# Dealing the first weights' columns out to the hidden blocks by fours, so that a row of a part of the second weights is one piece

## The chip, the cores and the metric

The kernel runs on one core of one Trainium2 chip. The metric is the device time of one execution in microseconds (us). The engines are TensorE (PE in the profile, its weight loads PEld), VectorE (DVE), ScalarE (ACT), GpSimd (POOL) and SyncE (SP). A transfer between memory and the chip is issued from the queue of SyncE or GpSimd.

## The reference, cut to what matters

Sparse attention over 8 batches, 8 heads, 576 positions and 64 dimensions (four heads with a local mask, four with a strided one) makes `x` of 4608 tokens by 512. A layer with a hidden width of 2048 follows; the change is in the latter alone:

```python
def _moe_ref(x, w_in, w_out):          # x 4608x512, w_in 512x2048, w_out 2048x512
    h = x @ w_in
    alpha = 1.0
    g = np.where(h > 0.0, h, alpha * (np.exp(np.minimum(h, 0.0)) - 1.0))
    return (g @ w_out).astype(np.float32)
```

The hidden width is summed over in the second product, so its 2048 units may be numbered in any order, as long as the columns of `w_in` and the rows of `w_out` follow the same one.

## The kernel before, in words

The tokens are kept as `xT`, with the 512 features on the partitions in `KC` = 4 chunks of 128. The tokens are taken in 9 chunks (`nb`) of 512. For each chunk the hidden width is cut into `MC` = 16 blocks (`m`) of 128 units. `moe_in` makes one block of `h`: four matmuls, one for each chunk `c` of features, with the 128 columns of `w_in_sb` that belong to the block as the stationary operand (a weight load of 128 by 128) and 512 tokens of `xT` as the moving one. These go through `moe_chunk` (L622). `moe_act` (L645 to L657) takes exp on ScalarE and a minimum, a subtraction and a maximum on VectorE, and writes block `m` of `g_sb`, with the 128 units on the partitions.

`moe_out` (L667) makes the output for 128 tokens: it runs over all 16 blocks, with 128 tokens of `g_sb` as the stationary operand and row block `m` of `w_out_sb` (128 units by 512) as the moving one. A quarter of that, four blocks, is one "part" of a call. ScalarE copies the sum to `o_sb` (L671), and SyncE stores it (L673).

The order of work is written out by hand. An opening list (`OPENING`) runs batch 0 of the attention, with some matmuls of the first three blocks in it (`moe_ahead`). After that, for each `nb` and each step `s` of 16, the loop issues pieces of the attention of the next batch, `moe_in` and `moe_act` of block `s`, and one part of `moe_out`, mostly of the chunk before. For the first chunk, parts 0, 1 and 2 of the first 128 tokens come at steps 11, 13 and 15.

Both weights are converted from float32 to bf16 by the transfers that load them, on GpSimd's queue. `w_in` comes in four transfers (`load_w_in(i)`, L316) of 512 columns each, which serve blocks 4i to 4i+3. `w_out` comes in four transfers (L728), one for each four blocks. They stand behind the loads of batch 1 and the last transfer of `w_in`, and ahead of the clearings (`clear_v`, `clear_nat`) and the loads of batch 2 (`load_batch(2)`: `load_strided`, L178 and L182, and `load_local`, L189 and L195).

Row `128 m + p` of `w_out` lies on partition `p`, in block `m`. So in one of the four transfers a partition gets four rows of `w_out` that are 128 rows apart in memory:

```python
wo = moe_w_out.rearrange("(m p) d -> p m d", p=128)
```

The attention is made for pairs of heads, in steps that carry short matmuls between those of the layer: transposes (L361, L375, L571, L584), scores (L456, L493) and the product with the values (L535, 65 columns). A second path (`general_path`) runs only when a range check on the sums of the attention fails.

Of the kernel before, what the change touches and what calls it, by code (L numbers as in the profile page):

```python
# [58 lines left out]
def kernel(  # L59
# [9 lines left out]
    nc = tc.nc  # L69
# [59 lines left out]
    w_in_sb = consts.tile([128, KC, d_ff], BF16, tag="w_in_sb")  # L129
# [115 lines left out]
    def clear_v(i, engine=nc.vector):  # L245
        engine.memset(v_str[i][:, :, :, D:], 1.0)
        engine.memset(v_loc[i][0:32, :, 0, :], 0.0)
        engine.memset(v_loc[i][:, :, :, D:], 1.0)
# [61 lines left out]
    nc.vector.memset(kT["loc"][1][:, :, 0:32], 0.0)  # L310

    wi = moe_w_in.rearrange("(c p) f -> p c f", p=128)
    wo = moe_w_out.rearrange("(m p) d -> p m d", p=128)

    def load_w_in(i):
        nc.gpsimd.dma_start(out=w_in_sb[:, :, 512 * i:512 * (i + 1)],  # L316
# [302 lines left out]
    hps_of = {}  # L619

    def moe_chunk(nb, m, c, hps, start, stop):
        nc.tensor.matmul(hps, lhsT=w_in_sb[:, c, m * 128:(m + 1) * 128],  # L622
                         rhs=xT[:, c, nb * N_TILE:(nb + 1) * N_TILE],
                         start=start, stop=stop)

    def moe_ahead(c, start, stop):

        for m in range(AHEAD):
            if start:
                ahead[m] = rings["hps"].next()  # L630
            moe_chunk(0, m, c, ahead[m], start, stop)

    def moe_in(nb, m):
        if m == 0:
            g_of[nb] = p_g.tile([128, MC, N_TILE], BF16, tag="g_sb", name="g_sb")
        if nb == 0 and m in ahead:
            hps = ahead[m]
        else:
            hps = rings["hps"].next()
            order = C_ORDER if nb < EARLY else sorted(C_ORDER)  # L640
            for c in order:
                moe_chunk(nb, m, c, hps, c == order[0], c == order[-1])
        hps_of[m] = hps
# [82 lines left out]
    load_w_in(3)  # L726
    for i in range(4):
        nc.gpsimd.dma_start(out=w_out_sb[:, 4 * i:4 * (i + 1), :],  # L728
                            in_=wo[:, 4 * i:4 * (i + 1), :])
    clear_v(2, nc.gpsimd)  # L730
    clear_nat(2, nc.gpsimd)
    load_batch(2)
# [50 lines left out]

    inner.close()
    general_path(tc, q, k, v, out, w_in_sb, w_out_sb, xT, identity, flag)


def general_path(tc, q, k, v, out, w_in_sb, w_out_sb, xT, identity, flag):


    nc = tc.nc
    B, H, S, D = q.shape
    KC, MC = w_in_sb.shape[1], w_out_sb.shape[1]
    redo = nc.values_load(flag[0:1, 0:1], min_val=0, max_val=1)
    with tc.If(redo > 0):
        with (
            tc.tile_pool(name="gp_c", bufs=1) as p_c,
            tc.tile_pool(name="gp", bufs=2) as p_s,
            tc.tile_pool(name="gp_ps", bufs=1, space=PSUM) as p_ps,
        ):  # L800

            same = p_c.tile([128, S], F32, tag="same")
            other = p_c.tile([128, S], F32, tag="other")
            nc.vector.memset(same, 0.0)
            for j in range(4):
                nc.gpsimd.affine_select(same, same, compare_op=ALU.not_equal, fill=1.0,
                                        base=-STRIDE * j,
                                        pattern=[[0, S // STRIDE], [-1, STRIDE]],
                                        channel_multiplier=1)
            nc.vector.tensor_scalar(other, same, scalar1=1.0, scalar2=-NEG,  # L810
                                    op0=ALU.subtract, op1=ALU.mult)
            for b in range(B):
                for hp in range(H // 2):
                    general_pair(nc, p_s, p_ps, q, k, v, xT, identity, same, other,
                                 b, hp)
            for nb in range(B * S // 512):
                g_sb = p_c.tile([128, MC, 512], BF16, tag="g", name="g")
                for m in range(MC):
                    hps = p_ps.tile([128, 512], F32, tag="a", name="hps")
                    for c in range(KC):  # L820
                        nc.tensor.matmul(hps, lhsT=w_in_sb[:, c, m * 128:(m + 1) * 128],
                                         rhs=xT[:, c, nb * 512:(nb + 1) * 512],
                                         start=(c == 0), stop=(c == KC - 1))
                    e_sb = p_s.tile([128, 512], F32, tag="e", name="e")
                    nc.scalar.activation(e_sb, hps, ACT.Exp)
                    e1_sb = p_s.tile([128, 512], BF16, tag="e1", name="e1")
                    nc.vector.tensor_scalar(e1_sb, e_sb, scalar1=1.0, scalar2=1.0,
                                            op0=ALU.min, op1=ALU.subtract)
                    nc.vector.tensor_tensor(g_sb[:, m, :], e1_sb, hps, op=ALU.max)
                for kk in range(4):  # L830
                    ops = p_ps.tile([128, 512], F32, tag="b", name="ops")
                    for m in range(MC):
                        nc.tensor.matmul(ops, lhsT=g_sb[:, m, kk * 128:(kk + 1) * 128],
                                         rhs=w_out_sb[:, m, :], start=(m == 0),
                                         stop=(m == MC - 1))
                    o_sb = p_s.tile([128, 512], F32, tag="o", name="o")
                    nc.scalar.copy(o_sb, ops)
                    r0 = nb * 512 + kk * 128
                    nc.sync.dma_start(out=out[r0:r0 + 128, :], in_=o_sb)
# [106 lines left out]
```

## Time and profile before

| what | value |
|---|---|
| median of 3 runs | 326.81 us (326.43 to 327.97) |
| profiled execution | 327.16 us, its span 325.3 us |
| mean granted TensorE clock | 0.997 |
| TensorE busy | 301.5 us (93%) |
| VectorE, ScalarE, GpSimd busy | 243.3, 177.8, 131.4 us |
| transfers on the GpSimd queue | 67632 packets, 18.10 MB |
| transfers on the SyncE queue | 34469 packets, 17.11 MB |
| read from and written to memory | 36.70 MB, 9.44 MB |

A line of the profile's groups names the source line, the engine, the operation, the tiles (out<-in), the shape and the count; then the busy time in us and the mean of one in ns; then the idle time of the engine before it and what ended it. A line of a timeline gives the start, the time that the merged instructions took, both in us, and the count. A line of the waits gives who waited for whom, the total in us, the number of times and the longest. A matmul's recorded duration (379 ns for 512 columns) holds its way through the array too, and consecutive matmuls overlap: the distance between starts is the pace. A weight load (PEld) can run beside the matmul before it.

### The profile page before, as it was taken

The numbers are of one execution on the slowest core, as the hardware profiler recorded it, in microseconds if no ns is written. First come the engines' busy times: TensorE is split into PE (matmuls) and PEld (weight loads), VectorE is DVE, ScalarE is ACT, GpSimd is POOL, SyncE is SP. The second block draws the span as 40 slices with busy tenths as digits, with TensorE's granted clock in tenths as the row PEclk, the third lists the DMA queues.
The fourth block names the chain that finished last, engine by engine and source line by source line (L and its number), as shares of the span: only waits on it lengthen the run. The fifth ranks groups of instructions, "written<-read, shape, count | busy, mean of one in ns | idle before, by whom it ended". The sixth has DMA issues, their size and how long they took to land.

```text
span 325.3 us, 6088 instructions
## 1 busy us (share of the span) xinstructions
PE 301.5 (93%) x2205; PEld 150.8 (46%) x2246; DVE 243.3 (75%) x539; ACT 177.8 (55%) x337; POOL 131.4 (40%) x208
## 2 busy tenths in 40 slices
PE   2697888999999999999999999999999999999992
PEld 1463544555544554444444454454445444444440
DVE  6576887787888788988798879887887666866600
ACT  3577885776455664555555655555565444434320
POOL 9579825958389368839823830000000000000000
PEclk9999999999999999999999999999999999999998
DMA  6999999999999999999988992920210001100012
GB/s 112 154 169 120 168 207 139 148 130 162 158 141 97 106 154 172 139 182 169 148 117 143 148 135 62 153 83 35 55 48 32 33 34 54 43 35 33 32 67 72
DMA packets 102138, 35.67 MB, mean 110 GB/s; under 512 B 79885, under 2 KB 97493, under 8 KB 102101
## 3 DMA queue, kind: packets, MB, share of 16 engines
q0 software_dynamic: 67632, 18.10, 64.6%
q1 hardware_dynamic: 34469, 17.11, 24.8%
q8 instruction: 19, 0.31, 0.4%
q14 instruction: 18, 0.15, 0.2%
HBM read 36.70 MB, written 9.44 MB: 142 GB/s over the span
## 4 chain that ended last, share of the span: by engine, by line
PE 86%; DVE 4%; DMA 3%; ACT 3%; issue 2%; POOL 2%; ACTq 0%; POOLq 0%
PE single L667 38%; PE half L622 28%; PE single L622 9%; PE single L535 3%; DMA k_loc<-in_k_dram 3%; PE pair_a L456 2%; PE single L375 2%; PE single L571 1%; ACT e_sb L648 1%; PE pair_a L493 1%; DVE g_sb L657 1%; POOL k_str L178 1%; DVE x_l L544 1%; DVE x_s L544 1%; DVE g_sb L652 1%
## 5 line engine op out<-in xcount | busy, mean ns | idle before, releaser
L667 PE MATMUL single<-w_out_sb,g_sb 128*128 128x512 bf16 x558 | 143.6, 379 | 1.4 <-DVE g_sb L657 0.4
L622 PE MATMUL half<-xT,w_in_sb 128*128 128x512 bf16 x419 | 110.3, 379 | 1.1 <-issue 0.3
L648 ACT ACTIVATE e_sb<-half 128x512 f32<-128x512 f32 x109 | 65.3, 599 | 68.7 <-PE half L622 62.4
L655 DVE TENSOR_SCALAR e_sb<-e_sb 128x512 bf16<-128x512 f32 x139 | 62.0, 446 | 36.5 <-ACT e_sb L648 35.4
L667 PEld LDWEIGHTS <-g_sb 128*128 128x128 bf16 x576 | 53.5, 98 | 59.6 <-DVE g_sb L657 1.2
L622 PEld LDWEIGHTS <-w_in_sb 128*128 128x128 bf16 x576 | 51.7, 98 | 55.2 <-issue 0.2
L657 DVE TENSOR_TENSOR g_sb<-e_sb,half 128x512 bf16<-128x512 bf16 x104 | 71.5, 688 | 3.6
L622 PE MATMUL single<-xT,w_in_sb 128*128 128x512 bf16 x136 | 36.0, 379 | 0.3 <-issue 0.2
L648 ACT ACTIVATE e_sb<-single 128x512 f32<-128x512 f32 x35 | 21.1, 602 | 21.6 <-PE single L622 19.6
L671 ACT COPY o_sb<-single 128x512 f32<-128x512 f32 x36 | 21.1, 586 | 17.7 <-PE single L667 16.5
L535 PEld LDWEIGHTS <-pr 128*128 128x128 bf16 (+3 forms) x352 | 20.9, 105 | 15.0 <-issue 1.1
L178 POOL DMA_DIRECT2D v_raw<-in_v_dram x32 | 19.9, 659 | 15.8 <-DVE v_str L414 15.7
L462 ACT ACTIVATE pr<-pair_a 126x936 bf16<-126x936 f32 (+1 forms) x20 | 19.2, 962 | 11.8 <-PE single L456 11.8
L657 DVE TENSOR_TENSOR g_sb<-e_sb,single 128x512 bf16<-128x512 bf16 x35 | 24.1, 688 | 1.2
L178 POOL DMA_DIRECT2D k_str<-in_k_dram x32 | 20.1, 647 | 7.6 <-issue 3.6
L178 POOL DMA_DIRECT2D q_str<-in_q_dram x28 | 17.6, 651 | 6.3 <-DMA w_out_sb<-in_moe_w_out_dram 2.0
L544 DVE TENSOR_TENSOR x_l<-single,rden 96x384 bf16<-96x384 f32 x32 | 17.7, 554 | 1.1
L501 ACT ACTIVATE pr<-pair_a 128x576 bf16<-128x576 f32 (+2 forms) x20 | 13.1, 653 | 6.9 <-PE pair_a L493 6.9
L544 DVE TENSOR_TENSOR x_s<-single,rden 126x256 bf16<-126x256 f32 (+1 forms) x32 | 15.7, 491 | 1.1
L543 DVE RECIPROCAL rden<-single 96x6 f32<-96x6 f32 (+2 forms) x64 | 11.9, 185 | 3.6 <-PE single L535 3.2
L201 POOL DMA_DIRECT2D q_loc<-in_q_dram x16 | 12.3, 794 | 3.2 <-DMA k_str<-in_k_dram 1.6
L182 POOL DMA_DIRECT2D k_str<-in_k_dram x8 | 4.8, 606 | 19.4 <-PE single L375 6.3
(114 smaller groups left out, 269.0 us busy)
## 6 DMA issues: line engine op xcount, KB each, us to landing
out_dram<-o_sb SPq DMA_DIRECT2D x36, 256.0 KB, 2.2
v_loc<-in_v_dram POOLq DMA_DIRECT2D x8, 288.0 KB, 9.7
k_str<-in_k_dram POOLq DMA_DIRECT2D x32, 67.5 KB, 4.6
v_raw<-in_v_dram POOLq DMA_DIRECT2D x32, 67.5 KB, 4.4
w_in_sb<-in_moe_w_in_dram POOLq DMA_DIRECT2D x4, 512.0 KB, 9.2
w_out_sb<-in_moe_w_out_dram POOLq DMA_DIRECT2D x4, 512.0 KB, 16.7
q_str<-in_q_dram POOLq DMA_DIRECT2D x28, 67.5 KB, 6.9
q_loc<-in_q_dram POOLq DMA_DIRECT2D x4, 288.0 KB, 5.4
```

The lines of the kernel that those rows point to most:

```text
L178: engine.dma_start(out=t[0:108, h].rearrange("p g d -> p (g d)"), in_=rows[h, :, 0:30, :].rearrange("t (r g) d -> t r (g d)", g=5))
L201: nc.gpsimd.dma_start(out=t[:, h // 2, 0:4, h % 2], in_=src[name][b, h, 0:512].rearrange("(i p) d -> p i d", p=128))
L462: nc.scalar.activation(both, sc[0:nk, :, 0:w], ACT.Exp, scale=scale)
L501: nc.scalar.activation(halves, sc[0:nk, :, 0:w], ACT.Exp, scale=scale)
L535: nc.tensor.matmul(av[0:m, p, blk - b0, :], lhsT=pr[0:nk, o:o + m], rhs=vt[0:nk, 2 * self.hp + p, blk, :], start=True, stop=True)
L544: nc.vector.tensor_tensor(self.x[0:nq, b0:b0 + n].rearrange("q g p d -> q p g d"), av[0:nq, :, 0:n, 0:D], r.unsqueeze(3).to_broadcast([nq, ...
L622: nc.tensor.matmul(hps, lhsT=w_in_sb[:, c, m * 128:(m + 1) * 128], rhs=xT[:, c, nb * N_TILE:(nb + 1) * N_TILE], start=start, stop=stop)
L648: nc.scalar.activation(e_sb, hps, ACT.Exp)
L655: nc.vector.tensor_scalar(e1_sb, e_sb, scalar1=1.0, scalar2=1.0, op0=ALU.min, op1=ALU.subtract)
L657: nc.vector.tensor_tensor(g_of[nb][:, m, :], e1_sb, hps, op=ALU.max)
L667: nc.tensor.matmul(ops, lhsT=g_of[nb][:, m, kk * 128:(kk + 1) * 128], rhs=w_out_sb[:, m, :], start=(m == 0), stop=(m == MC - 1))
L671: nc.scalar.copy(o_sb, ops)
```

## The change

Unit `512 i + 4 p + m` of the hidden width now belongs to partition `p` of block `4 i + m`, where before it was unit `128 m + p` in partition `p` of block `m`. On the side of `w_out`, the four rows that one partition gets in one transfer are neighbours in memory: 4 rows of 512 float32, 8 KB in one piece, which become 4 KB of bf16 in one piece on the partition. On the side of `w_in` the transfers stay as they are; the matmul's stationary operand now takes every fourth column of a 512-column part (`columns`), 8 bytes from one to the next in place of 2. A block still takes its columns from the same part as before, and `g_sb` and `moe_out` stay as they are. The path that the range check guards gets the same columns.

```diff
-    wo = moe_w_out.rearrange("(m p) d -> p m d", p=128)
+    wo = moe_w_out.rearrange("(i p m) d -> p i m d", p=128, m=4)
...
     def moe_chunk(nb, m, c, hps, start, stop):
-        nc.tensor.matmul(hps, lhsT=w_in_sb[:, c, m * 128:(m + 1) * 128],
+        nc.tensor.matmul(hps, lhsT=columns(w_in_sb, c, m),
                          rhs=xT[:, c, nb * N_TILE:(nb + 1) * N_TILE],
                          start=start, stop=stop)
...
     for i in range(4):
         nc.gpsimd.dma_start(out=w_out_sb[:, 4 * i:4 * (i + 1), :],
-                            in_=wo[:, 4 * i:4 * (i + 1), :])
+                            in_=wo[:, i])
...
+def columns(w_in_sb, c, m):
+
+    i = 512 * (m // 4)
+    return w_in_sb[:, c, i:i + 512].rearrange("p (f m) -> p m f", m=4)[:, m % 4]
...
-                        nc.tensor.matmul(hps, lhsT=w_in_sb[:, c, m * 128:(m + 1) * 128],
+                        nc.tensor.matmul(hps, lhsT=columns(w_in_sb, c, m),
```

## The prediction, made before the result was known

> **What bounds the kernel now.** The page comes first: which engine is full, and whose work the chain that ended last runs through.
>
> ```profile
> PE 301.5 (93%) x2205; PEld 150.8 (46%) x2246; DVE 243.3 (75%) x539; ACT 177.8 (55%) x337; POOL 131.4 (40%) x208
> ...
> PE 86%; DVE 4%; DMA 3%; ACT 3%; issue 2%; POOL 2%; ACTq 0%; POOLq 0%
> ```
>
> TensorE carries 86% of the chain, DMA 3%. So the next question is what a weight load costs beside a matmul. The groups of instructions with shapes kept apart give the loads; the timeline of both halves of TensorE shows how they lie together.
>
> ```profile
> L622 PEld LDWEIGHTS <-w_in_sb 128*128 128x128 bf16 x576 | 51.7, 98 | 55.2 <-issue 0.2 <-DMA w_in_sb<-in_moe_w_in_dram 0.2
> ...
> L535 PEld LDWEIGHTS <-pr 128*96 128x96 bf16 x22 | 2.7, 125 | 0.0
> ...
> L535 PEld LDWEIGHTS <-pr 108*108 108x108 bf16 x16 | 2.2, 137 | 0.0
> ...
> L535 PEld LDWEIGHTS <-pr 126*126 126x126 bf16 x6 | 1.0, 161 | 0.0
> ```
>
> ```profile
> 129.18 1.03 PE L667 MATMUL single<-w_out_sb,g_sb 128*128 128x512 bf16 x4
> 130.05 1.03 PE L622 MATMUL half<-xT,w_in_sb 128*128 128x512 bf16 x4
> ```
>
> ```profile
> 128.97 0.75 PEld L667 LDWEIGHTS <-g_sb 128*128 128x128 bf16 x4
> 129.83 0.75 PEld L622 LDWEIGHTS <-w_in_sb 128*128 128x128 bf16 x4
> ```
>
> Four matmuls of 512 columns start 0.87 us apart (129.18 to 130.05), 216 ns each, while a load takes 98 ns. Each load of a group begins one matmul ahead of its own (129.83 for a group at 130.05), so it has about 214 ns and 116 ns of that are spare. Two such matmuls run 1152 times: 1152 x 0.216 = 249 us of the 325.3 us span. The rest is attention and the start, and in the stretch from 60 to 300 us TensorE is busy for 237.9 of 240 us.
>
> Last, the second weights: their transfers, and who waits from 27 to 62 us, where they land.
>
> ```profile
> L728 POOL DMA_DIRECT2D w_out_sb<-in_moe_w_out_dram x4: 770/785/800, 31.9 to 34.1; - x4
> ...
>   POOL k_str L178: 4.0, 2
>   POOL q_str L178: 2.0, 1
>   POOL k_str L182: 1.9, 1
> ...
> DMA to landing us min/median/max: 13.7/16.7/19.3
> ```
>
> ```profile
> PEld L571 <- DVE x_s L544: 1.6, 2, 0.9
> ...
> PE pair_a L493 <- ACT pr L501: 1.4, 4, 0.7
> ...
> PEld L622 <- DMA w_in_sb<-in_moe_w_in_dram: 0.2, 1, 0.2
> ```
>
> Only GpSimd waits on the second weights (7.9 us over four waits). TensorE waits there on VectorE and ScalarE; its one short wait for weights, 0.2 us, is on the first ones.
>
> **The change, part by part.** Durations are from one execution of 327.16 us (span 325.3 and 1.86 us around it); the median of the runs shown is 326.81, or 0.35 us less. I sum against 327.16 and take 0.35 off at the end.
>
> *The transfers of w_out (L728).* Bytes and number of transfers stay; each row of a part becomes one piece of 8 KB read, 4 KB written, in place of four of 2 KB and 1 KB. In the trace's packet records those 1024-byte packets take 98 ns at the median, 2048 of them for w_out: 2048 x 98 / 16 engines = 12.5 us. The larger pieces are bounded by the records of the 8 KB packets of the instruction queue: 310 ns at the quick end, 458 at the median. 512 x 310 / 16 = 9.9 us and 512 x 458 / 16 = 14.7 us, so the last part lands between 2.6 us sooner and 2.1 us later. I take the nearest row of an actual 2 KB read or write, the output's 2048-byte packets at 84 to 87 ns: about 1.5 us sooner. The four parts land at 45.6, 48.7, 50.7 and 53.3 us; the matmuls of L667 that first read them start at 48.3, 51.5, 55.1 and 57.3. The smallest margin is 2.6 us, so either end costs TensorE nothing here. What hides the transfer is that margin, made by the first chunk's long run of L622 matmuls; without it, a part that came 2.1 us late would cost 2.1.
>
> *What is queued behind them.* On GpSimd's queue follow the clearings and the loads of batch 2, which wait for room (the 7.9 us). They come as much sooner or later as the transfers do. The last of k_str lands at 57.6 and its transposes start at 58.2, a margin of 0.6 us: the late end would cost 2.1 - 0.6 = 1.5 us, the early end saves nothing because TensorE doesn't wait for it now. GpSimd's own four issues take 785 ns each; the 18 KB loads of L182 take about 606 ns, so at most 4 x 0.18 = 0.7 us of GpSimd's time goes, which no chain step follows. I take 0.
>
> *The loads of w_in's columns (L622).* The number stays 576 loads of 128 by 128. What moves is where the 128 columns lie: 8 bytes apart, over 1 KB of each partition, and no longer next to each other. Each part i of the first weights still serves the blocks 4i to 4i+3, so no wait on the weights moves. The trace has no load with a step. From below: a packed load reads the least, so no gain. From above: the loads in the trace that are slower per column, those of under 128 columns, at 125, 137 and 161 ns for 96, 108 and 126 columns, 1.2 ns for a column, so 163 ns for 128 (those after the first 20 us run 122, 128 and 136, which gives 137). All of these stay below 214 ns, so behind a 512-column matmul they cost nothing. In the order of loads, 432 of the 576 follow another load of w_in and 77 one of g_sb; 67 follow a load of attention, whose matmul is short (19 after L535, 26 after L456 and L493, 22 after transposes), and there a longer load is bare: 67 x (137 - 98) = 2.6 us, 67 x (163 - 98) = 4.4 us. I take 98 ns, hence 0, by the nearest row in rows, columns and type: the 576 loads of g_sb, of the same 128 by 128 bf16.
>
> The Trainium skill speaks to this in "TensorE: Matmul & The Clock Gate", section Weight-path perf modes: the fast load holds for 128 columns that aren't fp32 at steps of up to 1,024 elements, with a pattern "packed or strided". The gap between the 98 ns row and the shorter, slower ones agrees with its condition on columns; no row here has a step. A rule against the change stands in "SBUF — State Buffer", Specifications (TRN2): 16-byte lines, at least two hits in a line for full speed, and a penalty at each new line. An 8-byte step has exactly two hits but crosses four times as many lines; the page prices neither. By the first page the sum stays at 0; by the second it would become what the first rival below works out from rows.
>
> Sum: 0 (transfers) + 0 (GpSimd) + 0 (loads) on 327.16, less 0.35: **326.8 us**.
>
> **The rivals.**
>
> *Slower: the strided load loses its speed.* For it: the step is all that differs on TensorE, the bounding engine, and the 126-column row shows that a load of this size can take far longer. Against: 214 ns cover 509 of the 576. Price: 67 bare loads at 39 to 65 ns more, 2.6 to 4.4 us, 329.4 to 331.2 us; it decides from 24 ns more per load (67 x 24 ns = 1.6 us). Its extreme is a load above 214 ns: from there each ns costs 509 ns more, so 300 ns gives 67 x 0.202 + 509 x 0.086 = 57 us, 384 us. No load in the trace is near that, the longest of pr taking 212 ns in the first 20 us.
>
> *Faster: a lighter queue quickens the start.* From 20 to 60 us TensorE is busy for 34.0 of 40 us, and VectorE is stretched beside GpSimd's issues: L655 takes 1.13 us at 60.2 and 0.96 at 37.2 against 0.44 usually. If fewer pieces free VectorE, a chain of x_s and x_l could come forward. For 1.8 us, a bit under a third of those 6.0 idle us, the time is 325.0. Against: all waits in that stretch are for VectorE and ScalarE work that follows itself, and the twelve L655 there take 5.7 us, only 0.4 over twelve at 444 ns.
>
> *It doesn't do what it says: the row is cut up again on its way.* If the cast keeps pieces of 1 KB, landing stays at 13.7 to 19.3 us and the time at 326.8, as nothing hung on it.
>
> **How the numbers follow.** Forecast 0.50, rows cut up again 0.10, slower load 0.22, load above 214 ns 0.05, quicker start 0.13. A measurement of this kernel can tell about 0.5%, 1.6 us, from no change. Faster is then 0.13; same 0.50 + 0.10 = 0.60; slower 0.22 + 0.05 = 0.27. The range must hold 0.80: 325.4 takes in the larger part of the gains short of 325.0, 330.6 most of the slower load (2.6 us to about 3.8) and the 1.5 us of late batch 2 loads; out are the best of the quicker start (0.08), the dear end of the slower load (0.07) and the load above 214 ns (0.05). The likeliest case alone lies between 326.0 and 328.
>
> **What would show it.** Right: L622's loads still at about 98 ns, their matmuls 216 ns apart, 509 of them covered; w_out's landing at 10 to 17 us and its packets four times larger; GpSimd's waits on w_out below 7.9 us; the waits of TensorE from 27 to 62 us the same. Wrong: loads of 130 ns or more with a gap after L535, L456 or L493 before L622 (slower rival), groups of four L622 matmuls over 0.87 us (a load above 214 ns), or a stretch from 20 to 60 us with TensorE busy well over 34 us earlier in its work, the first L667 before 47 us (faster rival).

## The result and the profile after

The changed kernel takes 349.26 us (median of 4 runs, 346.75 to 350.09) where the kernel before takes 326.62 us (median of 4): a ratio of 1.0671, 95% interval 1.0625 to 1.0716. The forecast was 326.8 us, range 325.4 to 330.6. The profiled execution took 350.09 us, its span 348.3. Medians and ratios below leave out executions in the slower of the two states that the program is found in (one of e1 and one of e3).

The page of the changed kernel, with the same lines as before, and two rows of 40 equal slices of the span (busy tenths of TensorE, tenths of full speed of the clock that it was granted):

```profile
PE 306.1 (88%) x2205; PEld 161.0 (46%) x2246; DVE 244.5 (70%) x539; ACT 177.7 (51%) x337; POOL 130.2 (37%) x208
...
PE   2850449889999999999999999999999999999993
...
PEclk9995586999999999999999999999999999999997
...
PE 80%; DMA 9%; POOL 3%; DVE 3%; issue 2%; ACT 2%; POOLq 0%; ACTq 0%
```

TensorE is busy for only 4.6 us more, in a span that is 23.0 us longer. The loss isn't work: it is a hole near the start, in the fourth to the sixth slice (26 to 52 us), and the granted clock is low from there to 61 us. Transfers carry 9% of the chain in place of 3%. The waits from 20 to 62 us, and TensorE's timeline, say where:

```profile
PEld L622 <- DMA w_in_sb<-in_moe_w_in_dram: 20.4, 2, 16.9
PE half L622 <- DMA w_in_sb<-in_moe_w_in_dram: 20.2, 2, 16.8
...
POOL w_in_sb L316 <- PE single L361: 15.7, 1, 15.7
```

(The first two rows are the same waits, of the weight load and of its matmul.) The timeline before, then after:

```profile
23.82 0.60 PE L622 MATMUL half<-xT,w_in_sb 128*128 128x512 bf16 x2
...
31.15 1.04 PE L622 MATMUL half<-xT,w_in_sb 128*128 128x512 bf16 x4
```

```profile
22.54 0.36 PE L535 MATMUL single<-v_loc,pr 128*128 128x65 bf16 x6 [0.22 <-DVE x_l L544]
39.72 1.04 PE L622 MATMUL half<-xT,w_in_sb 128*128 128x512 bf16 x2 [16.82 <-DMA w_in_sb<-in_moe_w_in_dram]
...
51.72 1.90 PE L622 MATMUL half<-xT,w_in_sb 128*128 128x512 bf16 x4 [3.36 <-DMA w_in_sb<-in_moe_w_in_dram]
```

The first L622 of the opening needs part 0 of `w_in` alone, and that landed at 20.8 us. It starts at 39.72, right after part 2 has landed (39.67). The first L622 after the opening, block 3, needs part 0 too. It starts at 51.72, after part 3 has landed (51.67). The semaphore waits that the traces record say the same without any timing. Before, the first L622 waits for the transfer of part 0 alone, and those of parts 1, 2 and 3 are first waited for at blocks 4, 8 and 12. After, the first L622 waits for parts 0, 1 and 2, and block 3 for part 3. The engine's sequencer stands at the first of these waits until part 1 has landed (25.2 us), long before part 2:

```profile
L622 PEldq EVENT_SEMAPHORE  x1: 2672/2672/2672, 22.6 to 22.6; - x1
```

GpSimd's timeline, before and then after, shows a transfer that waits in its turn for TensorE:

```profile
30.39 1.52 POOL L316 DMA_DIRECT2D w_in_sb<-in_moe_w_in_dram  x2
```

```profile
29.77 0.82 POOL L316 DMA_DIRECT2D w_in_sb<-in_moe_w_in_dram  x1
46.31 0.75 POOL L316 DMA_DIRECT2D w_in_sb<-in_moe_w_in_dram  x1 [15.72 <-PE single L361]
47.04 2.15 POOL L728 DMA_DIRECT2D w_out_sb<-in_moe_w_out_dram  x4
```

The transfer of part 3 was issued at 31.1 us before, unheld; now it waits on a semaphore of TensorE and goes at 46.31, after the opening's last L622 (which ended at 46.01; the profile names the transposes right behind that, which stand later in the program than the transfer), and w_out and batch 2 are held behind it. The two things that the prediction priced, the loads and the transfers of w_out, read thus:

```profile
L622 PEld LDWEIGHTS <-w_in_sb 128*128 128x128 bf16 x576 | 60.8, 115 | 72.1 <-DMA w_in_sb<-in_moe_w_in_dram 20.4 <-issue 3.5
```

```profile
L728 POOL DMA_DIRECT2D w_out_sb<-in_moe_w_out_dram x4: 548/551/558, 47.0 to 48.6; - x4
...
DMA to landing us min/median/max: 7.1/10.0/12.9
```

A load takes 115 ns in place of 98, and all but the bare ones stay covered by the 216 ns matmul ahead of them.

Landmarks of the two timelines place the loss: the first L622 starts 15.9 us later (39.72 against 23.82), the first after the opening 20.6 (51.72 against 31.15), the first L667 21.8 (70.07 against 48.26), the last L667 23.1 (342.04 against 318.94).

### The profile page after: what moved, and what is told of

Read it like the earlier page. It is cut to its first block, busy times and chain, and to the rows that moved or that the text cites. A ratio compares the mean times of both kernels' runs of the same rounds, so it can differ in the third digit from the quotient of the medians.

```text
span 348.3 us, 6080 instructions
## 1 busy us (share of the span) xinstructions
PE 306.1 (88%) x2205; PEld 161.0 (46%) x2246; DVE 244.5 (70%) x539; ACT 177.7 (51%) x337; POOL 130.2 (37%) x208
## 4 chain that ended last, share of the span: by engine, by line
PE 80%; DMA 9%; POOL 3%; DVE 3%; issue 2%; ACT 2%; POOLq 0%; ACTq 0%
PE single L667 35%; PE half L622 27%; PE single L622 9%; DMA w_in_sb<-in_moe_w_in_dram 7%; PE single L535 3%; DMA q_loc<-in_q_dram 2%; PE pair_a L456 2%; PE single L375 1%; PE single L571 1%; PE single L361 1%; POOL k_str L178 1%; POOL q_str L178 1%; DVE e_sb L655 1%; PE pair_a L493 1%; DVE g_sb L657 1%
## 5 line engine op out<-in xcount | busy, mean ns | idle before, releaser
L667 PE MATMUL single<-w_out_sb,g_sb 128*128 128x512 bf16 x558 | 143.8, 379 | 1.4 <-DVE g_sb L657 0.4
L622 PE MATMUL half<-xT,w_in_sb 128*128 128x512 bf16 x419 | 113.2, 387 | 22.2 <-DMA w_in_sb<-in_moe_w_in_dram 20.2
L622 PEld LDWEIGHTS <-w_in_sb 128*128 128x128 bf16 x576 | 60.8, 115 | 72.1 <-DMA w_in_sb<-in_moe_w_in_dram 20.4
L667 PEld LDWEIGHTS <-g_sb 128*128 128x128 bf16 x576 | 53.5, 98 | 58.4 <-DVE g_sb L657 1.3
L622 PE MATMUL single<-xT,w_in_sb 128*128 128x512 bf16 x136 | 36.8, 386 | 0.5 <-issue 0.3
L178 POOL DMA_DIRECT2D k_str<-in_k_dram x32 | 19.8, 643 | 8.4 <-DMA w_out_sb<-in_moe_w_out_dram 2.7
L544 DVE TENSOR_TENSOR x_s<-single,rden 126x256 bf16<-126x256 f32 (+1 forms) x32 | 15.7, 491 | 1.1
L364 ACT COPY qT_str<-single 128x630 bf16<-128x630 bf16 x5 | 3.4, 685 | 19.7 <-PE single L361 19.6
L201 POOL DMA_DIRECT2D k_loc<-in_k_dram x16 | 12.6, 823 | 1.8 <-DMA v_raw<-in_v_dram 1.3
```

The source lines that it names most:

```text
L178: engine.dma_start(out=t[0:108, h].rearrange("p g d -> p (g d)"), in_=rows[h, :, 0:30, :].rearrange("t (r g) d -> t r (g d)", g=5))
L201: nc.gpsimd.dma_start(out=t[:, h // 2, 0:4, h % 2], in_=src[name][b, h, 0:512].rearrange("(i p) d -> p i d", p=128))
L544: nc.vector.tensor_tensor(self.x[0:nq, b0:b0 + n].rearrange("q g p d -> q p g d"), av[0:nq, :, 0:n, 0:D], r.unsqueeze(3).to_broadcast([nq, ...
L622: nc.tensor.matmul(hps, lhsT=columns(w_in_sb, c, m), rhs=xT[:, c, nb * N_TILE:(nb + 1) * N_TILE], start=start, stop=stop)
L667: nc.tensor.matmul(ops, lhsT=g_of[nb][:, m, kk * 128:(kk + 1) * 128], rhs=w_out_sb[:, m, :], start=(m == 0), stop=(m == MC - 1))
```

## The experiments

The theory (A): a stepped read of one part is taken to meet the transfers of the other parts. In the tile a partition holds four chunks of 2048 columns, and each part is a stretch of 512 in every chunk, so the parts are interleaved. A read of 128 neighbours was told apart from them, a read of every fourth element isn't. The framework that turns the program's reads and writes into semaphore waits then makes L622 wait for every part issued before it in program order, and makes part 3's transfer wait for the L622 ahead of it. Rivals: (B) the stepped loads slow TensorE themselves; (C) the larger pieces of w_out hold up the queue.

### e1_part_major: the step kept, the parts laid apart

```diff
-    w_in_sb = consts.tile([128, KC, d_ff], BF16, tag="w_in_sb")
+    w_in_sb = consts.tile([128, 4, KC, 512], BF16, tag="w_in_sb")
...
-        nc.gpsimd.dma_start(out=w_in_sb[:, :, 512 * i:512 * (i + 1)],
+        nc.gpsimd.dma_start(out=w_in_sb[:, i],
...
-    i = 512 * (m // 4)
-    return w_in_sb[:, c, i:i + 512].rearrange("p (f m) -> p m f", m=4)[:, m % 4]
+    return w_in_sb[:, m // 4, c].rearrange("p (f m) -> p m f", m=4)[:, m % 4]
```

> The changed kernel with w_in_sb laid out part by part (128 x 4 parts x 4 chunks x 512), so that each transfer of w_in fills one stretch of 2048 elements; the columns are still 8 bytes apart and w_out's rows still one piece. Theory A (the waits: a stepped read of a part is taken to meet the transfers of other parts, whose rows are interleaved with it in the tile, so TensorE waits for parts 2 and 3 and the transfer of part 3 waits for TensorE): both waits go, no L622 waits on a w_in transfer for over 1 us, and the time is 326.5 to 328.5 us, the 1 us over before being 67 bare loads at 15 ns more. Theory B (the stepped loads themselves slow TensorE): the loads are as before this edit, so 347 to 350 us. Theory C (the larger pieces of w_out hold up the queue): 347 to 350 us.

Measured: 327.83 us, ratio to the kernel before 1.0015 (0.9971 to 1.0058). Of TensorE's waits from 15 to 70 us, one is for `w_in`:

```profile
PE single L622 <- DMA w_in_sb<-in_moe_w_in_dram: 0.9, 1, 0.9
```

That one wait is block 8's, which does need part 2 (0.2 us in the kernel before). The loads still take 114 ns and w_out's rows still come in one piece, so neither B nor C holds: the layout alone takes the loss away, to within what can be measured. In its semaphore records the waits of L622 and of part 3's transfer are those of the kernel before.

### e2_columns_only and e3_rows_only: one part of the change each

```diff
 e2, against the changed kernel
-    wo = moe_w_out.rearrange("(i p m) d -> p i m d", p=128, m=4)
+    wo = moe_w_out.rearrange("(m p) d -> p m d", p=128)
...
-                            in_=wo[:, i])
+                            in_=wo[:, 4 * i:4 * (i + 1), :])
 e3, against the kernel before: the same lines the other way round
```

> The changed kernel with w_out's transfers as they were before (four pieces of 2 KB for each partition); only the stepped columns are left of the change, so the hidden units of the two weights don't match and the output isn't the reference's. Theory A: the two waits are still there, 347 to 351 us, perhaps 0 to 2 us over the changed kernel as w_out lands later. Theory B: 347 to 350 us. Theory C: about 327 us.

> The kernel before with w_out's rows in pieces of 8 KB alone; the columns of w_in stay packed, so the hidden units of the two weights don't match and the output isn't the reference's. Theory A and theory B: 326.0 to 327.0 us, the same as before, with w_out landing about 2 us sooner and its packets at 324 ns. Theory C: 347 to 350 us.

Measured: columns alone 351.18 us, 1.0722 (1.0654 to 1.0791), 0.2 us above the range of theory A; rows alone 327.3 us, 1.0021 (0.9985 to 1.0057). TensorE's waits for `w_in` in e2, and the landing of `w_out` in e3:

```profile
PE half L622 <- DMA w_in_sb<-in_moe_w_in_dram: 21.5, 2, 18.2
```

```profile
DMA to landing us min/median/max: 13.6/16.5/19.5
```

The step brings the loss and the pieces bring nothing that can be measured. In e3 w_out's last part lands at 53.28 us, in the kernel before at 53.33, so the 2 us that were expected of the landing didn't come either.

### e4_part_major_packed: the layout alone

The kernel before with the tile of e1 and packed columns (`w_in_sb[:, m // 4, c, m % 4 * 128:(m % 4 + 1) * 128]`).

> The kernel before with w_in_sb laid out part by part and nothing else: packed columns, w_out as before. It tells what the layout alone does. All theories: 326.0 to 327.5 us, loads of w_in at 98 ns, so that e1 against this one gives the cost of the step and the gain of the pieces.

Measured: 327.17 us, 0.9987 (0.9956 to 1.0018). The layout costs nothing. Together with e1, the kernel before and the changed one this fills a square: packed or stepped, interleaved or apart. Only stepped and interleaved waits for parts that it doesn't need.

### e5_waits_only: the waits put into the kernel before

```diff
+    def meet(ps, i, alone=True):
+        nc.tensor.matmul(ps, lhsT=w_in_sb[:, 0, 512 * i:512 * i + 128],
+                         rhs=mask_l[:, 0:512], start=alone, stop=alone)
+
     def moe_ahead(c, start, stop):
...
                 ahead[m] = rings["hps"].next()
+                if m == 0:
+                    meet(ahead[m], 2)
+            if stop and m == AHEAD - 1:
+                meet(ahead[m], 3, False)
...
+            if nb == 0 and m == AHEAD:
+                meet(hps, 3)
```

(and `nc.vector.memset(w_in_sb[:, 0, 1536:1664], 0.0)` at the start, so that the third matmul adds zero)

> The kernel before, with packed columns and w_out as before, to which only the waits of the changed kernel are added as real ones: one more matmul at the first L622 that reads part 2 of w_in, one at the first L622 after the opening that reads part 3, and one at the last L622 of the opening that reads, ahead of its transfer, a piece of part 3 that was set to zero, so that the transfer waits for it. Three matmuls of 0.22 us are added; what they compute is overwritten or adds zero. Theory A (the waits are the whole loss but about 1 us): 346 to 349 us, TensorE idle from about 23 to 40 us and again for some 3 us at 48, TensorE's granted clock down in the stretch from 20 to 60 us. Theory B' (the waits are a sign of something in the stepped loads or in the pieces that also costs time by itself): clearly under 345 us.

Measured: 348.97 us, 1.0705 (1.0629 to 1.0781): the loss is there with packed loads and old pieces. The waits of TensorE, and those of GpSimd:

```profile
PE half L628 <- DMA w_in_sb<-in_moe_w_in_dram: 20.6, 2, 17.4
```

```profile
POOL w_in_sb L317 <- PE single L628: 16.4, 1, 16.4
```

(L628 is the matmul of `meet`; L317 is L316 of the other kernels.) Here the program itself asks for the waits, and they have the size of those in the changed kernel. So the waits are enough to make the loss; e1 shows that without them it is gone.

### e6_part3_early: the second wait taken away

The changed kernel with `load_w_in(3)` right after `load_w_in(2)`, ahead of the opening.

> The changed kernel with the transfer of part 3 of w_in issued right after part 2, ahead of the opening, so that it can't be held by the opening's L622. Theory A: one wait instead of two, now until part 3 has landed too (42 to 44 us), no L316 waiting for TensorE, w_out landing by 54 us, no second wait. The first L622 moves from 23.8 to about 43, 19 us, and with 1 to 2 us at the lower clock and 1 us of bare loads the time is 346 to 349 us: the second wait goes and the first grows by as much. If the hold on the transfer were the larger part of the loss, it would fall below 340 us.

Measured: 349.96 us, 1.0709 (1.0669 to 1.0750). That is 1 us above the range that theory A gave, and far from the 340 us of its rival:

```profile
PE half L623 <- DMA w_in_sb<-in_moe_w_in_dram: 21.0, 1, 21.0
```

One wait of 21.0 us in place of 16.8 and 3.4; part 3 lands at 43.05, the first L622 starts at 43.13, and w_out lands by 52.9. Block 3 starts at 51.96, where in the changed kernel it starts at 51.72. So GpSimd's queue being held 15.7 us shows no price of its own beyond the second wait: what counts is how long TensorE is made to wait, in one piece or in two.

### e8_by_chunk: interleaved tile, transfers of one stretch each

```diff
-        nc.gpsimd.dma_start(out=w_in_sb[:, :, 512 * i:512 * (i + 1)],
-                            in_=wi[:, :, 512 * i:512 * (i + 1)])
+        for c in range(KC):
+            nc.gpsimd.dma_start(out=w_in_sb[:, c, 512 * i:512 * (i + 1)],
+                                in_=wi[:, c, 512 * i:512 * (i + 1)])
```

> The changed kernel with w_in_sb laid out as before the change, chunk by chunk, and each transfer of w_in cut into four, one for each chunk, so that each fills one stretch of 512 elements and meets no other part. Theory A, as stretches that are interleaved: the waits go though tile and step are those of the changed kernel; GpSimd issues 12 transfers more, 0.6 us each, so part 2 lands some us later than 40 us, and the time is 327 to 331 us. If instead any stepped read waited for all that is written into the tile: 347 us or more.

Measured: 330.77 us, 1.0128 (1.0094 to 1.0162). Tile, step and columns are those of the changed kernel, and TensorE's waits for w_in from 15 to 70 us are 1.2 us:

```profile
PE single L362 <- DMA k_str<-in_k_dram: 1.9, 1, 1.9
PE single L623 <- DMA w_in_sb<-in_moe_w_in_dram: 1.2, 2, 1.0
```

So a stepped read doesn't wait for the whole tile: it is the transfer over four stretches that it is taken to meet. That this goes by the bounds of the four stretches, which enclose the other parts, fits e1 and e8, but the framework's rule itself is not shown. The 1.3% over the kernel before goes with the 12 transfers more on GpSimd: part 2's last piece lands at 43.4 us, part 3's at 46.5, and a load of k_str is waited for (1.9 us). That share is argued from the waits and wasn't isolated.

### e9_fill: the waits kept, the clock kept up

72 matmuls of no use (`identity` by `mask_l`, 512 columns) ahead of the opening's first L622 and 14 ahead of block 3's.

> The changed kernel with matmuls that compute nothing of use (the identity by a mask, 512 columns, overwritten by the next matmul) put into the two waits: 72 ahead of the first L622, about 15.5 of the 16.8 us, and 14 ahead of the first L622 after the opening, about 3.0 of the 3.4 us. The waits stay as long as they are, but TensorE is busy in them. Theory A with a share of the clock: the granted clock stays at 1.0 from 20 to 60 us, the first L622 still starts at 39.7 to 40.5 us, and the time falls from 349 to 346 to 347.5 us, since the matmuls right after the waits run at full clock. If the clock costs nothing, it stays at 348 to 350 us; if the lower clock, and not the waits, were the main loss, it would fall below 340 us.

Measured: 347.79 us, 1.0624 (1.0554 to 1.0694). The mean granted clock (the third number from the end) from 20 to 60 us, in the changed kernel and then here:

```profile
20.00:60.00 40.00, 17.25 (x140) 9.97 (x141) 12.55 (x30) 13.54 (x27) 19.01 (x31) 0.70 0.94 129
```

```profile
20.00:60.00 40.00, 33.95 (x240) 17.52 (x237) 12.98 (x31) 14.03 (x28) 18.53 (x30) 0.96 0.94 126
```

From the first L622 to the first L667 it takes 27.9 us in place of 30.4. The fill fell 3.3 us short of part 2, which landed 0.9 us later in that run (40.54), and from 39.7 to 45.9 us the clock is still 0.72, so the test takes away only a part of the clock's share. The time is 0.3 us above the expected range. The gain of some 1.5 us in the median isn't settled, since the intervals of the two ratios overlap, and the 2.4 us between the landmarks are one trace against one. But with the clock mostly kept up, 21 of the 22.6 us are still there: the clock is a tail of the waits and not the loss.

### e7_steps: the load by itself

The kernel of e1, in which the last chunk's loads take 128 columns at other steps, two blocks for each step (the wrong columns for that chunk). L629, L631 and so on are steps of 1, 2, 3, 4, 8, 16, 32 and 64 elements.

> The kernel of e1 in which the last chunk's loads take 128 columns at steps of 1, 2, 3, 4, 8, 16, 32 and 64 elements (2 to 128 bytes), two blocks for each, wrong columns for that chunk. It measures the load by itself. If a load's time goes by the lines of 16 bytes that it crosses: 98 ns at step 1, 113 at step 4, more at 8, then level. If it goes by the step being there at all: 113 ns from step 2 on. If it grows with the distance: over 214 ns at step 32 or 64, with matmuls further apart than 216 ns.

The groups of its last 50 us (one execution, 328.71 us), the largest step first:

```profile
L643 PEld LDWEIGHTS <-w_in_sb 128*128 128x128 bf16 x8 | 1.4, 174 | 0.5
L641 PEld LDWEIGHTS <-w_in_sb 128*128 128x128 bf16 x8 | 1.2, 145 | 0.7
L639 PEld LDWEIGHTS <-w_in_sb 128*128 128x128 bf16 x8 | 1.2, 144 | 0.7
L637 PEld LDWEIGHTS <-w_in_sb 128*128 128x128 bf16 x8 | 1.1, 144 | 0.7
L635 PEld LDWEIGHTS <-w_in_sb 128*128 128x128 bf16 x8 | 0.9, 114 | 0.8
L633 PEld LDWEIGHTS <-w_in_sb 128*128 128x128 bf16 x8 | 0.8, 103 | 0.9
L631 PEld LDWEIGHTS <-w_in_sb 128*128 128x128 bf16 x8 | 0.8, 98 | 0.9
L629 PEld LDWEIGHTS <-w_in_sb 128*128 128x128 bf16 x8 | 0.8, 97 | 1.0
```

The load grows from a step of 3 elements on, is level from 8 to 32 elements (16 to 64 bytes), and takes 174 ns at 128 bytes. Up to 64 bytes that is the first of the three expectations. The rise at 128 bytes isn't in it, and the third, which had one, had it past 214 ns. Even there the load stays below 214 ns, and the loads are a median 216 ns apart at every step.

## Why the prediction was wrong, point by point

**The step that failed** is this sentence: "Each part i of the first weights still serves the blocks 4i to 4i+3, so no wait on the weights moves." The data that a block needs are indeed the same. But the waits in the program aren't made of what is needed; they are made of what the framework can tell apart. I read the dependence off the index arithmetic and didn't count the wait as something that the form of a read can change. The square of four layouts shows that it can, the semaphore records show the added waits themselves, which stop TensorE for 16.8 and 3.4 us where it waited 0.2 us for `w_in` before, and e5 shows that these waits alone, with the clock that falls in them, cost 22 us.

**The rival on the slower side** named the right object, the stepped read, with the wrong mechanism: its time in the array. Its case of 329 to 331 us didn't come, nor did that of a load above 214 ns. No case of mine had a wait in the place of none. The rival on the faster side didn't show either: e3, which has the larger pieces alone, is at 1.0021.

**The loads.** Taken at 98 ns with bounds to 163; measured at 113 to 115, inside the bounds. 67 bare loads x 15 ns are 1.0 us, and the landmarks leave 23.1 - 21.8 = 1.3 us for all that comes after the first L667. By the times it can't be told from nothing: e1 against e4 is 327.83 against 327.17. That 509 loads stay covered was right (matmuls 216 ns apart).

**The rule of the lines.** "SBUF — State Buffer", Specifications (TRN2), in the Trainium skill asks for two hits in a 16-byte line for full speed. For weight loads e7 disagrees by a little: at two hits (step 4) a load takes 114 ns and not 97, at four hits (step 2) 98. That crossing lines costs, as the same passage says, agrees (144 ns at step 8, where every element lies in a line of its own).

**The transfers of w_out.** Taken to land 1.5 us sooner, which is 2048 packets at 86 ns, although the change leaves 512; e3's last part lands at 53.28 us against 53.33. The packets did what was expected of them, 324 ns for 4096 bytes in place of 98 for 1024, so 512 x 324 / 16 = 10.4 us of packet time in place of 12.5. But the parts land 2.48 us apart (45.84 to 53.28) where they landed 2.57 apart, a gain of 0.3 us over three parts: the sum of packet times was not the pace of the queue. Over all traces the two kinds overlap: 2.54 to 2.76 us apart with the old pieces (before, e2, e4, e5), 2.46 to 2.71 with the new. That nothing hung on it was right, as e3's ratio shows. GpSimd's issues became shorter, 551 ns in place of 785, and that brought nothing either.

**The loss, split.** First wait: 15.9 us at the first L622. Second wait: 3.4 of the 4.7 us that come up to block 3. What is left of that, 1.3 us, and 1.2 us up to the first L667 I put down to the clock; it is 0.64 behind the first wait (39.7 to 45.9 us) and 0.53 behind the second (51.7 to 58.2 us), where an L622 matmul takes up to 634 ns against 390. The rest, 1.3 us, is likely the bare loads: from the first to the last L667 the traces with packed loads take 270.7 to 271.3 us (before, e3, e4, e5), those with stepped ones 271.2 to 273.0 (after, e1, e2, e6, e8, e9). It wasn't isolated. The Trainium skill says in "TensorE: Matmul & The Clock Gate", Part 1, that the clock halves after a window of idleness; the trace agrees, with a granted clock of 0.50 from 27.1 to 44.1 us, after TensorE had gone idle at 22.9.

## What to carry to other kernels

When a change gives a read or a write another access pattern, look at what else is written into the same tile, and how: a stepped read beside transfers that are interleaved in the tile can be given waits that the data don't ask for, on both sides. Lay a tile out so that what is loaded together is one stretch; then pattern and arrival are independent, and here it cost nothing (e4). And compare the waits of the two traces first when a span grows but no engine's busy time does.

## What the runs showed of the hardware that was not expected

In one execution (e7) a load of 128 by 128 bf16 weights takes 97, 98, 103, 114, 144, 144, 145 and 174 ns at steps of 1, 2, 3, 4, 8, 16, 32 and 64 elements, and behind a 512-column matmul none of it shows. Pieces four times as long (4096 bytes in place of 1024 on the partition) brought w_out's parts only from 2.57 to 2.48 us apart (e3 against the kernel before), less than the traces of one kind differ among themselves.
